# When an even chunk's k and v loads are issued in an mLSTM-plus-FFN kernel: behind the odd chunk's section, or behind the product of W's last column with v

## The chip, the core and the metric

The kernel runs on one core of a Trainium2 chip. The metric is the device time of one execution in microseconds (us). Five engines work side by side, each through its own instructions in order: TensorE (PE, with its weight loads listed as PEld), VectorE (DVE), ScalarE (ACT), GpSimd (POOL) and SyncE (SP). SP, POOL and ACT also issue DMAs, each through a queue of its own; an issue stands in the engine's order like any other instruction.

## The reference

Two blocks follow each other. The first is an mLSTM cell over 4 batches, 8 heads, 768 tokens and a head size of 40:

```python
for t in range(S):
    m_new = np.maximum(f_gate[:, :, t] + m, i_gate[:, :, t])
    f_stab = np.exp(f_gate[:, :, t] + m - m_new)
    i_stab = np.exp(i_gate[:, :, t] - m_new)
    C = f_stab * C + i_stab * outer(v_t, k_t)
    n = f_stab * n + i_stab * k_t
    y_t = sigmoid(o_gate_t) * (C @ q_t) / max(|n . q_t|, 1)
```

The second takes y as 3072 rows of 320 numbers: `h = max(x @ w_in, 0)`, then `(h * h) @ w_out`, with w_in of 320 x 2048 and w_out of 2048 x 320. All in float32.

## The kernel before

**Chunks and groups.** The attention is done in 24 chunks of 128 tokens (six to a batch, all heads at once), numbered s; c is s modulo 6. Two chunks make one group g of 256 token rows for the FFN, so there are 12 groups. In the steady part (the loop of lines 1437 to 1612) each stage has four steps, `at` = 0 to 3. In an even stage s the second FFN product of an old group runs (`ffn2_fast`, line 1063, the matmuls of L1058); in an odd stage s the first FFN product of a later group runs in two halves (`ffn1_open`, `ffn1_close` and `ffn1_rows`, lines 1142, 1175 and 1158; matmuls L1137 and L1170). The attention of the chunks is threaded between them. The order on every engine is the order in which the program writes its instructions, since a manual schedule is set (line 87); nothing reorders them.

**One half of the first FFN product.** It uses four PSUM tiles X, Y, V and Z. `ffn1_open` fills X (L1150), Y, V and Z; ACT copies X (L1151), DVE adds that to Y (L1153, "r_sb") and then V to the sum (L1155). `ffn1_close` adds a second product to X and then writes new products over Y and V; in the second half (`at` = 3) these start afresh, so PE may write Y only when L1153 has read it, and V only when L1155 has.

**The attention of an even chunk s+1 inside odd stage s, from chunk 10 on** (`joined`). All of it comes at `at` = 2, between the two halves of the FFN product, and just behind: `weigh` lets ACT turn the masked decays A into the weights W, eight activations of L510, and then calls `values`: POOL multiplies v by the last column of W into vw (L531), which the state update needs. `weighted` then lets DVE multiply the scores by W, in place (two instructions of L609); the product is written over W, so it waits until POOL has read W's last column. Next on DVE come L1153 and L1155 of the half that was just opened, then `scale_q` (L763) and `turn_kq` (L406, a transpose). The matmuls of the chunk (`attend_begin`: L801, L821, L832) stand on PE between V's second product and the rows of L1170.

There is no vw in a batch's last chunk (c = 5), and no decay of a state in its first (c = 0).

**POOL in an odd stage.** In order: the causal mask of chunk s+1 (two L479) and the decay of the state (`decay_C`, L768, "Cd"), both at `at` = 1; then k and v of chunk s+3 (`load`, seven DMAs: L363, two of L365, four of L375), for s above `EARLY` = 10; vw of chunk s+1 (L531); eight DMAs that copy k and q of two later chunks into rows of a DRAM buffer (`pair_up`, L343; four in stage 19); k and v of chunk s+4 (seven DMAs again). Then in even stage s+1: mask and Cd of chunk s+2, vw of chunk s+2, and four subtractions and additions of x (`sums_of_x`, L1129 and L1132). DMAs of the POOL queue use eight semaphores in turn, so each waits, before it is issued, until the DMA eight places before it has landed.

**Buffers.** There are four buffers each for k and q (`kq_b`) and v (`va_b`), used in turn, so chunk s+3 is loaded into the buffers of chunk s-1. The loads of even chunks 14 to 22, those that the change touches, wait for no engine in the built program, only for their semaphore. Chunk s+3's v is first read in stage s+2.

Of the kernel before, what the change touches and what calls it, by code (L numbers as in the profile page):

```python
# [29 lines left out]
def kernel(  # L30
# [317 lines left out]
    def load(s):  # L348
        b, c = divmod(s, NB)
        (dk, sk), nat_q, vv = load_parts(s)  # L350
        if s < ROT:
            for dst, src in ((dk, sk), nat_q, vv) if s < KQ_SQ else ((dk, sk), vv):
                nc.sync.dma_start(dst, src[b, :, c * P : (c + 1) * P, :].rearrange("h p d -> p h d"))
            return
        load_k(s)
        load_v(s)
# [35 lines left out]
    def load_squares(s, eng=None):  # L392

        eng = eng or nc.sync
        t = kqT(s)[:].rearrange("p n j (m a) -> p (n j m) a", a=SQ)
        for i in range(2):
            for e in range(0, D, SQ):
                w = min(SQ, D - e)
                eng.dma_start(
                    t[DP * i + e : DP * i + e + SQ, :, :w],  # L400
                    kq_d[s, i, :, :, :, e : e + w].rearrange("n j (m r) a -> r (n j m) a", r=SQ),
                )
# [5 lines left out]
    def load_o(s):  # L408
        b, c = divmod(s, NB)
        r, (s0, s1) = next((r, (a, z)) for r, (a, z) in enumerate(RUNS) if a <= s < z)  # L410
        if s == s0:
            st["og", r] = ld.tile([P, 4, H, D], F32, name="og")
        og = st.setdefault(s, {})["og"] = st["og", r][:, s - s0]
        nc.sync.dma_start(og, o_gate[b, :, c * P : (c + 1) * P, :].rearrange("h p d -> p h d"))
# [151 lines left out]
    def scores(s, o=(False, False)):  # L566
        d = st[s]

        sc = [bank(o[i]) for i in range(2)]
        d["sc"] = sc  # L570
        if s >= KQ_SQ:
            if s >= ROT:
                d["sc"] = [t.rearrange("p j t -> p (j t)")[:, : 3 * P].rearrange("p (e t) -> p e t", e=2) for t in sc]
            for e in range(2):
                for late_keys in range(2):
                    for c in range(2):
                        for i in range(2):
                            rows = slice(DP * i, DP * i + D)
                            start = e == late_keys == 0
                            if s < ROT:  # L580
                                j, keys = 2 * late_keys + e, HALVES[c]
                                to, t0 = sc[i][HALVES[c], j, :], 0
                            else:
                                j, keys = 2 * (c ^ late_keys) + e, HALVES[late_keys]
                                to = d["sc"][i][HALVES[c], e, slice(0, DP) if late_keys else slice(DP, 3 * DP)]
                                t0 = DP * late_keys
                            nc.tensor.matmul(  # L587
                                to, lhsT=d["kT"][rows, j, keys], rhs=d["qT"][rows, j, t0:], start=start, stop=True,
                                skip_group_check=True,
                            )  # L590
            return
        for j in range(PR):
            for i in range(2):
                rows = slice(DP * i, DP * i + D)
                nc.tensor.matmul(
                    sc[i][:, j, :], lhsT=d["kT"][rows, j, :], rhs=d["qT"][rows, j, :], start=True, stop=True,
                )
# [328 lines left out]
    def store_rows(s):  # L926
        t = st[s]["xT"] = xT_half(s).rearrange("p c t -> p (c t)")
        nc.sync.dma_start(x_d[s].rearrange("c t d -> t c d"), st[s]["x"][:].rearrange("p (c d) -> p c d", c=3))

    def load_rows(s):  # L930
        t = st[s]["xT"]
        for r in range(P // SQ):
            nc.sync.dma_start(
                t[r * SQ : (r + 1) * SQ].rearrange("p (b a) -> p b a", a=SQ),
                x_d[s, :, :, r * SQ : (r + 1) * SQ].rearrange("c (n p) a -> p (c n) a", p=SQ),
            )

    def turn_squares(s):
        t = st[s]["xT"]
        nc.vector.transpose(t, t)  # L940
        del st[s]
# [86 lines left out]
    def sums_of_weights(i):  # L1028
        if i < 3:
            T[i] = late.tile([P, NPAIR, DH], F32, name=f"T{i}", bufs=1)[:]  # L1030
        if i == 0:
            nc.vector.tensor_tensor(T[0], B12, B11, op=ALU.subtract)
        elif i == 1:
            nc.vector.tensor_tensor(T[1], B22, T[0], op=ALU.subtract)
        elif i == 2:
            nc.vector.tensor_tensor(T[2], B21, T[1], op=ALU.subtract)
        else:

            nc.vector.tensor_tensor(B12, B22, B12, op=ALU.subtract)
# [118 lines left out]
    def ffn1_rows(g, q, first):  # L1158
        xT, xs = st["xT", g], st["xs"]
        X, Y, V, Z = st["f1"]  # L1160
        lo, hi = HALVES
        pairs = (
            ((X, lo, xT[lo, 0, 2, :], False), (Y, hi, xT[hi, 1, 2, :], first)),
            ((V, lo, xT[lo, 1, 2, :], first), (Z, hi, xs[hi, 1, :], False)),
        )
        for pair in pairs:
            for n in range(4):
                for cols in HALVES:
                    for to, rows, rhs, start in pair:
                        nc.tensor.matmul(  # L1170
                            to[cols, n, :], lhsT=w_in2[rows, 4 * q + n, cols], rhs=rhs,
                            start=(start and n == 0), stop=True, skip_group_check=True,
                        )
# [36 lines left out]
    def do(f, s):  # L1210
        if 0 <= s < NT:
            f(s)
# [97 lines left out]
    for u in range(8):  # L1310
        s = 2 + u // 2
# [119 lines left out]
    EARLY = 10  # L1431
    assert ROUNDED[-1] == len(pieces)

    def joined(s):
        return EARLY <= s < NT and s % 2 == 0

    for n, (which, g, i) in enumerate(parts):
        s, at = NB + n // 4, n % 4
# [3 lines left out]
        even = s % 2 == 0  # L1442
# [17 lines left out]
        if at == (0 if joined(s) else 1):  # L1460
            if not joined(s):
                do(attend_begin, s)
            if n == 5:
                sums_of_weights(3)
            if even:
                do(lambda s: scores(s, ("h" if s < EARLY else False, "h")), s + 1)
            if fast:
                ffn1_rows(g, 0, True)
                if joined(s + 1):
                    scores(s + 1, (False, "h"))  # L1470
            do(attend_end, s)
            do(decays, s + 1)
            if not even and s + 2 > EARLY:
                do(lambda s: load_squares(s, nc.scalar), s + 2)
                if s > EARLY + 1:
                    do(half_tanh, s)
            do(mask, s + 1)
            if not even and not fast:
                do(turn_kq, s + 1)
            do(decay_C, s + 1)  # L1480
            if not fast and not even:
                do(turn_squares, s - 1)
            if s == NB + 2:
                load(s + 3)
            if not even and s > EARLY:
                do(load, s + 3)
            do(store_num, s)
            if s > NB + 1:
                do(load_A, s + 2)
            if joined(s):  # L1490
                load_rows(s - 1)
            if n == 1:
                normalise_turned(5)
                store_rows(5)
                turn_squares(4)
            if n == 5:
                load_rows(6)
            do(load_num, s)
            if n == 1:
                load_rows(5)  # L1500
                weigh(7, masked=True)
                sums_of_win(2)
            if s + 2 <= EARLY:
                do(load_squares, s + 2)
            if even and s <= NB + 1:
                do(load_A, s + 2)
# [87 lines left out]
        if n in (5, 6):  # L1594
            load(4 + n)
            load_o(5 + n)
        if at == 3 and s == NB + 2 or at == 2 and joined(s + 1):
            for r in (3, 4) if even else (4, 5):
                do(pair_up, s + r)
# [43 lines left out]
```

## Time and profile before

| | us |
|---|---|
| median of 3 runs | 493.96 (492.89 to 493.99) |
| the profiled execution, its own time | 492.39 |
| its span, first to last instruction | 490.7 |
| outside the span | 1.69 |
| PE busy | 474.2 (97% of the span) |
| PEld busy | 442.6 (90%) |
| DVE busy | 346.3 (71%) |
| ACT busy | 243.6 (50%) |
| POOL busy | 223.1 (45%) |
| granted TensorE clock | 1.000 |

All times of an instruction are counted from the span's start. The views used are: the page's shares and its groups by line; the list of waits of one engine (who waited for whom, total us, times, longest); the chain of work that ended last, in order of time; and the timelines of single engines. In a timeline a row has start, duration, engine, line, operation, output<-input and count, and in brackets the idle time before it and what ended that. The odd stages that the change touches lie at about these times, by their weigh activations (L510) on ACT: stage 11 at 191.1, 13 at 227.8, 15 at 266.3, 17 at 304.8 and 19 at 341.9 us.

### The profile page before, as it was taken

What the parts mean: (1) busy time and instruction counts of PE and PEld (TensorE: products, weight loads), DVE (VectorE), ACT (ScalarE), POOL (GpSimd) and SP (SyncE); (2) the same over time, 40 slices, a digit from 0 to 9 for tenths busy, and PEclk for the clock granted to TensorE, in tenths of its full rate; (3) what the DMA queues carried; (4) which work ended last, traced back from release to release, by engine and by line L of the source; (5) the groups of instructions that cost most, each with busy time, mean ns of one, the idle gap of its engine ahead of it and who ended that gap; (6) DMA issues with size and microseconds to landing.
All of it is one profiled execution on the core that took longest, in us unless ns stands there. A gap on an engine that the chain in (4) does not pass through costs nothing.

```text
span 490.7 us, 15678 instructions
## 1 busy us (share of the span) xinstructions
PE 474.2 (97%) x6389; PEld 442.6 (90%) x6389; DVE 346.3 (71%) x725; ACT 243.6 (50%) x534; POOL 223.1 (45%) x337
## 2 busy tenths in 40 slices
PE   8989999999999999999899899999899999999997
PEld 4876787789998999999899899899899999999997
DVE  7868868898975966864966867856866867735441
ACT  4698898636645424545345453554552651514300
POOL 5464454658598735735834825824832111020000
PEclk9999999999999999999999999999999999999999
DMA  8999998689999848767867867855954322200000
GB/s 177 231 242 267 254 231 219 189 149 199 164 198 200 158 128 173 158 127 154 146 146 150 156 147 124 189 132 112 179 126 88 89 76 73 56 23 15 2 28 27
DMA packets 192839, 69.93 MB, mean 143 GB/s; under 512 B 158144, under 2 KB 181504, under 8 KB 192768
## 3 DMA queue, kind: packets, MB, share of 16 engines
q1 hardware_dynamic: 157424, 56.39, 51.9%
q0 software_dynamic: 6080, 10.16, 9.7%
q10 hardware_dynamic: 29264, 2.39, 4.5%
q8 instruction: 50, 0.82, 0.8%
q14 instruction: 21, 0.17, 0.2%
HBM read 55.69 MB, written 18.92 MB: 152 GB/s over the span
## 4 chain that ended last, share of the span: by engine, by line
PE 73%; DMA 8%; DVE 6%; POOL 4%; SPq 3%; issue 3%; ACT 2%; DVEq 0%; POOLq 0%; ACTq 0%
PE h_ps L1058 31%; PE h_ps L1137 16%; PE h_ps L1170 7%; PE h_ps L974 4%; PE h_ps L1012 4%; PE numT L821 3%; DMA kqT<-kq_rows 2%; PE numT L801 2%; POOL va L375 1%; PE tp L587 1%; DMA x_rows<-x_sb 1%; PE numT L832 1%; DMA lent_t<-in_moe_w_in_dram 1%; DMA num_rows<-tn 1%; PE h_ps L985 1%
## 5 line engine op out<-in xcount | busy, mean ns | idle before, releaser
L1074 DVE TENSOR_TENSOR y_sb<-y_sb,h_ps 128x160 f32<-128x160 f32 x44 | 13.8, 314 | 53.7 <-PE h_ps L1058 53.7
L1058 PE MATMUL h_ps<-T,S 128*128 128x160 f32 x352 | 51.4, 299 | 0.0
L1058 PE MATMUL h_ps<-w_out,g 128*128 128x160 f32 x336 | 48.9, 301 | 0.9 <-issue 0.9
L1058 PEld LDWEIGHTS h_ps<-T,S 128*128 128x128 f32 x352 | 49.0, 190 | 0.0
L1058 PEld LDWEIGHTS h_ps<-w_out,g 128*128 128x128 f32 x336 | 46.2, 190 | 2.1 <-issue 1.7
L1137 PE MATMUL h_ps<-lent_t,w_in 128*128 128x128 f32 x320 | 42.7, 276 | 5.0 <-DVE r_sb L1153 5.0
L1137 PEld LDWEIGHTS h_ps<-lent_t,w_in 128*128 128x128 f32 x320 | 38.9, 192 | 5.7 <-DVE r_sb L1153 5.7
L1151 ACT COPY r_sb<-h_ps 128x512 f32<-128x512 f32 x20 | 11.7, 584 | 65.1 <-PE h_ps L1137 65.1
L1137 PE MATMUL h_ps<-xT,w_in 128*128 128x128 f32 x320 | 43.3, 278 | 0.0
L1170 PE MATMUL h_ps<-xT,w_in 64*64 64x128 f32 x960 | 40.3, 272 | 1.4 <-DVE r_sb L1153 1.4
L1129 POOL TENSOR_TENSOR lent_t<-xT 128x128 f32<-128x128 f32 (+1 forms) x18 | 10.3, 592 | 67.0 <-DVE xT L940 67.0
L1137 PEld LDWEIGHTS h_ps<-xT,w_in 128*128 128x128 f32 x320 | 39.2, 192 | 1.6 <-issue 1.2
L375 POOL DMA_DIRECT2D va<-in_v_dram x64 | 39.2, 622 | 0.1
L1137 PE MATMUL h_ps<-lent_t 128*128 128x128 f32 x320 | 39.0, 275 | 0.0
L1170 PEld LDWEIGHTS h_ps<-xT,w_in 64*64 64x64 f32 x960 | 35.4, 133 | 2.6 <-DVE r_sb L1153 2.1
L1137 PEld LDWEIGHTS h_ps<-lent_t 128*128 128x128 f32 x320 | 37.3, 192 | 0.0
L510 ACT ACTIVATE A_bc<-A_bc,b_R 128x64 f32<-128x64 f32 (+1 forms) x128 | 35.6, 363 | 0.9 <-POOL A_bc L479 0.9
L479 POOL TENSOR_SCALAR_AFFINE_SELECT A_bc<-A_bc 64x512 f32<-64x512 f32 x32 | 23.6, 736 | 23.6 <-ACT kq L497 22.3
L1188 ACT ACTIVATE g<-h_ps 128x512 f32<-128x512 f32 x12 | 7.2, 597 | 49.2 <-PE h_ps L1170 19.5
L768 POOL TENSOR_TENSOR Cd<-C,kq 128x164 f32<-128x164 f32 x15 | 13.9, 929 | 36.2 <-DVE C L862 31.6
L974 PE MATMUL h_ps<-xT,w_in 128*128 128x256 f32 x128 | 29.9, 386 | 0.4 <-POOL w_in L236 0.4
L855 DVE STREAM_TRANSPOSE tn<-numT 128x256 f32<-128x256 f32 x36 | 14.0, 426 | 22.9 <-PE numT L801 15.7
(231 smaller groups left out, 1210.1 us busy)
## 6 DMA issues: line engine op xcount, KB each, us to landing
A_bc<-a_slots SPq DMA_DIRECT2D x32, 256.0 KB, 5.0
kq<-num_rows SPq DMA_DIRECT2D x80, 64.0 KB, 3.1
num_rows<-tn SPq DMA_DIRECT2D x18, 256.0 KB, 2.9
raw<-in_moe_w_out_dram SPq DMA_DIRECT2D x7, 640.0 KB, 4.7
og<-in_o_gate_dram SPq DMA_DIRECT2D x24, 160.0 KB, 4.9
x_rows<-x_sb SPq DMA_DIRECT2D x20, 192.0 KB, 2.7
xT<-x_rows SPq DMA_DIRECT2D x80, 48.0 KB, 3.5
out_dram<-y_sb SPq DMA_DIRECT2D x23, 160.0 KB, 2.3
```

What stands on the lines that cost most here:

```text
L375: eng.dma_start(dst[HALVES[n], PR * (1 - late_keys) : PR * (2 - late_keys)], src[HALVES[late_keys], PR * m : PR * (m + 1)],)
L479: nc.gpsimd.affine_select(part, part, compare_op=ALU.is_ge, fill=-1e30, base=0, pattern=[[0, PR], [0, 2], [1, DP]], channel_multiplier=-1,)
L510: nc.scalar.activation(A[0][:, x, to], A[0][:, x, to], AF.Exp, bias=b_R[:, b, c, own, x : x + 1],)
L768: nc.gpsimd.tensor_tensor(Cd, C_b[(s - 1) % 2][:, : PR * D1].rearrange("p (j d) -> p j d", d=D1), st[s]["eA"][:, :, P - 1 : P].to_broadcas ...
L821: nc.tensor.matmul(d["numT"][m][HALVES[e], i, t0:], lhsT=va_w[s % NKQ][keys, at * D1 : at * D1 + DP], rhs=rhs, start=(s % NB == 0 and i == ...
L855: nc.vector.transpose(to[:, 2 * m : 2 * m + 2], d["numT"][m].rearrange("p c t -> p (c t)"))
L974: nc.tensor.matmul(hs[i][:, n, :], lhsT=w_in[:, a, fb * P : (fb + 1) * P], rhs=xT[:, :, a, :], start=(n == 0 and a == 0), stop=False,)
L1012: nc.tensor.matmul(st["o_ps"][j], lhsT=st["g2", 0][:, fb, j * P : (j + 1) * P], rhs=w_out[:, fb, :], start=(fb == 0), stop=(fb == NF - 1),)
L1058: nc.tensor.matmul(to, lhsT=lhsT[:, p], rhs=rhs[:, p, :], start=(start and p == 0), stop=(p == NPAIR - 1), skip_group_check=True,)
L1074: add = lambda to, a, b: nc.vector.tensor_tensor(to, a, b, op=ALU.add)
L1137: nc.tensor.matmul(to[:, n, :], lhsT=lhsT[:, 4 * q + n, :], rhs=rhs, start=(start and n == 0), stop=True, skip_group_check=True,)
L1170: nc.tensor.matmul(to[cols, n, :], lhsT=w_in2[rows, 4 * q + n, cols], rhs=rhs, start=(start and n == 0), stop=True, skip_group_check=True,)
```

## The change

In odd stages above 10 the call that loads k and v of chunk s+3 moves from `at` = 1 (behind mask and Cd of chunk s+1) to the end of `at` = 2, behind vw of chunk s+1 and ahead of the copies of `pair_up`. It holds for s = 11, 13, 15, 17 and 19, that is for the chunks 14, 16, 18, 20 and 22.

```diff
             if s == NB + 2:
                 load(s + 3)
-            if not even and s > EARLY:
-                do(load, s + 3)
             do(store_num, s)
...
         if n in (5, 6):
             load(4 + n)
             load_o(5 + n)
+        if at == 2 and not even and s > EARLY:
+            do(load, s + 3)
         if at == 3 and s == NB + 2 or at == 2 and joined(s + 1):
             for r in (3, 4) if even else (4, 5):
                 do(pair_up, s + r)
```

The instructions of PE, DVE, ACT and SP keep their order. On POOL one instruction changes places with seven, five times:

```diff
 L768 TensorTensor Cd<-C_1208,kq_94 128x164
-L363 DMACopy kq_92<-in_k_dram 128x4x40
-L365 DMACopy kq_92<-in_k_dram 64x4x40 x2
-L375 DMACopy va_96<-in_v_dram 64x4x40 x4
-L531 TensorTensor vw<-va_98,A_bc 128x328
+L531 TensorTensor vw<-va_98,A_bc 128x328
+L363 DMACopy kq_92<-in_k_dram 128x4x40
+L365 DMACopy kq_92<-in_k_dram 64x4x40 x2
+L375 DMACopy va_96<-in_v_dram 64x4x40 x4
 L343 DMACopy kq_rows<-in_k_dram 16x4x320 x2
 L343 DMACopy kq_rows<-in_q_dram 16x4x320 x2
```

The order of POOL's DMAs among themselves is the same, and so are the semaphores that they use.

## The prediction

> **What bounds the kernel now.** I read the page's shares first, then who makes PE wait in the steady part, then who makes that engine wait, then the chain.
>
> ```profile
> PE 474.2 (97%) x6389; PEld 442.6 (90%) x6389; DVE 346.3 (71%) x725; ACT 243.6 (50%) x534; POOL 223.1 (45%) x337
> ```
>
> PE is busy 97% of the span, with a full granted clock, so time is won only where PE stands still. The waits of PE and of DVE between 150 and 400 us:
>
> ```profile
> PE h_ps L1137 <- DVE r_sb L1153: 5.0, 4, 1.3
> ```
> ```profile
> DVE A_bc L609 <- POOL vw L531: 5.9, 3, 2.0
> ```
>
> PE waits four times for L1153, the DVE instruction that reads Y. In three of the four, DVE itself stood about 2 us in front of L609 until POOL had made vw. The chain of waits shows what POOL did meanwhile, here in stage 13:
>
> ```profile
> 227.44 0.46 POOL Cd L768
> 227.90 0.79 POOL kq L363
> 228.69 1.23 POOL kq L365 x2
> 229.91 2.43 POOL va L375 x4
> 232.36 0.77 POOL vw L531
> 233.19 0.44 issue
> 233.62 0.55 DVE A_bc L609
> 234.17 0.61 DVE r_sb L1153
> 234.82 2.05 PE h_ps L1137 x16
> ```
>
> It issued the seven loads that the change moves, 4.46 us, while W was ready long before vw began: ACT's timeline has the last L510 done at 227.82 + 2.22 = 230.04. The same chain stands at 265.96 (stage 15) and 341.56 (stage 19). Stages 11 and 17 differ: their chunk is a batch's first, no Cd holds the loads back, and ACT is last. POOL's timeline of stage 17:
>
> ```profile
> 297.82 0.80 POOL L363 DMA_DIRECT2D kq<-in_k_dram  x1 [0.50 <-issue]
> 298.62 1.23 POOL L365 DMA_DIRECT2D kq<-in_k_dram  x2
> 299.84 2.45 POOL L375 DMA_DIRECT2D va<-in_v_dram  x4
> 307.20 0.74 POOL L531 TENSOR_TENSOR vw<-va,A_bc 128x328 f32<-128x328 f32 x1 [4.92 <-ACT A_bc L510]
> ```
>
> These two stages are my model of the changed ones: vw starts 0.14 us behind ACT (304.84 + 2.22 = 307.06), L609 goes on right behind DVE's L940, and PE has no gap there.
>
> **What the change takes away, stage 13.** POOL is free after Cd at 227.90, ACT ready at 230.04, so vw starts at 230.18 and ends at 230.92 (0.74, as in stage 17). DVE is busy until then: L1192 at 230.02, L940 at 230.62 to 231.19; in stage 17 L609 starts 0.49 us after L940 starts, so here at 231.11, not 233.15. L1153, 0.94 us behind it in stage 13 (234.09 - 233.15), starts at 232.05 and ends at 232.73. PE's second Y may begin one block, 0.90 us, behind the second X at 232.48, that is at 233.38; L1153 is 0.65 us early. L1155, 0.78 us behind L1153, ends at 233.52; the second V needs it at 234.27. L763, 1.39 us behind L1153, ends at 234.12; the chunk's matmuls (L801) need it at 236.81 - 1.55 = 235.26. Nothing on DVE is late next.
>
> **Price of the stall.** On PE's timeline, from the start of the second X to the start of the second V:
>
> ```profile
> 309.50 1.06 PE L1137 MATMUL h_ps<-xT,w_in 128*128 128x128 f32 x8
> 310.40 1.06 PE L1137 MATMUL h_ps<-lent_t,w_in 128*128 128x128 f32 x8
> 311.29 1.06 PE L1137 MATMUL h_ps<-xT,lent_t 128*128 128x128 f32 x8
> ```
>
> 1.79 us in stage 17, without a stall. In stage 13 it is 235.82 - 232.48 = 3.34, in stage 15 274.35 - 270.98 = 3.37, in stage 19 349.94 - 346.58 = 3.36. The stalls cost 1.55 + 1.58 + 1.57 = 4.70 us. Stages 11 and 17 give 0: vw cannot be earlier than ACT.
>
> **What the change puts later.** On POOL the seven issues (4.47 us) now stand behind vw, and behind them, as before, the eight `pair_up` copies, the seven loads of chunk s+4, and mask and Cd of chunk s+2. The other queues (SP's and ACT's) are passed by nothing. The even chunk's data is late for nobody: chunk 16's last issue would end at 235.4 instead of 232.3, at most 7.4 us to landing (the longest of the 64 v loads) makes 242.8, and vw of chunk 16 reads it near 270. The rows of `pair_up` in stage 13 are first read back in stage 15, near 258.
>
> What could be late is the mask, since each copy waits for the DMA eight places before it. In stage 13 of before the sixth copy started at 236.72, released by the landing of the second v load, issued by 231.1: 5.6 us to land. I use that for all, as these stages are the busy ones for DMA. Stage 11, the tightest: vw ends at 193.49 + 0.74 = 194.23; loads 4.47, to 198.7; the eighth copy waits for the last load, to 204.3, and takes 0.51; loads of chunk 15 4.44, to 209.3; mask 1.56, to 210.8, against 204.8 before. ACT would like to start L510 of chunk 13 at 209.29, so it is 1.7 us late there. But its 2.23, 0.14 and a slow vw of 1.21 bring vw to 214.5, and DVE takes up L609 of chunk 13 at 216.36: 1.8 us of slack left, cost 0. Even with 7.4 us to land the mask ends at 212.6 and vw at 216.3.
>
> The others have more, with PE's earlier times taken off: stage 13's mask ends at 247.5 (before 244.4), L609 of chunk 15 is due at 255.56 - 1.55 = 254.0, and 247.5 + 0.14 + 2.23 + 0.14 + 1.21 = 251.2 leaves 2.8. Stage 17 ends its mask 6.6 us later than before but keeps about 3; stages 15 (next chunk has no vw) and 19 (four copies, not eight) keep 4 or more. So this costs 0 as long as landings stay below about 7.5 us.
>
> Two bounds are open. **vw's own time** beside a busy DVE: L531 took 738 to 1206 ns. At 1.21 it ends at 231.39, L1153 at 233.06, still 0.3 early: cost 0. The longest vw in the trace, 1.76 us (the form of L537), would put L1153 at 233.6, 0.25 late, or 0.75 us in three stages. **The issues** beside a busy DVE: 64 L375 took 617 to 654 ns while DVE was busy 71%, so I take no stretch.
>
> A rule speaks against this last point. The Trainium skill, "SBUF — State Buffer", section "A bandwidth-pool intuition that's wrong (but worth ruling out)", has a DMA issued by GpSimd take about 3.1 us instead of 0.62 beside a VectorE copy that holds their shared port. The loads move from beside an idle DVE to beside a busy one. By that rule one such issue in a stage, 2.5 us longer, would eat stage 12's 1.8 us and cost 0.7, making the sum -4.0 us. This trace shows no stretched issue.
>
> **Sum.** -4.70 + 0 + 0 = -4.7 us. The profiled execution took 492.39 in its own time (span 490.7), which becomes 487.7. The median of the runs is 493.96, 1.57 above it; I forecast for a median: **489.3 us**. The spread of the three runs (1.1 us), below and above, with a few tenths for small shifts elsewhere, makes its own range 487.6 to 490.6. About 0.3% (1.5 us) is what a measurement of this kernel can tell from no change.
>
> **Rivals.**
>
> *Part of the gain is given back* (chance 0.08): vw is slower than 1.2 us beside DVE, or the delayed mask holds ACT in stage 12 alone. For it: the slow vws stand beside DVE work, and stage 12's slack is the smallest. Against: at 1.21 and at 7.4 us both are still covered. Price: 0.75 us by the 1.76 row, up to 2.5 us with landings near 10 us in one stage: 490.0 to 491.8.
>
> *Nothing is won: the wait for vw isn't the cause* (chance 0.08). L609 would next wait for another thing that came at nearly the same time (the scores, or a DMA behind L940), as in the fourth L1153 stall at 159.65, where vw was done at 156.93 and DVE went on late only behind L940, released by the DMA of xT. For it: that one case. Against: in all three stages L940 was done 2 us before vw and the profile names vw. Two of three stalls staying leaves -1.6; all three, 0: 492.4 to 494.
>
> *Slower: POOL's shifted queue holds the even stages* (chance 0.04). Place: the mask of chunks 13, 15, 19 and 21, then L510, vw and L609 in stages 12, 14, 18 and 20. Point: landings 1.8 us above 5.6 in stage 12, about 3 above in stages 14 and 18. From there each us is a us of PE. At 10 us to landing, 4.4 above, that is 2.6 + 1.6 + 1.4 + 0 = 5.6 against 4.7 won: 494.9; at 12 us, 4.6 + 3.6 + 3.4 = 11.6, 500.9. Against it: the longest landing of a v load is 7.4 and their median 4.2.
>
> **Numbers.** The forecast has 0.80. The range, 487.6 to 491.8, takes the forecast and the first rival: 0.88, some of it cut at the tails. Both lie below 493.96 - 1.48 = 492.48, so faster has 0.88; the second rival is what lies within 0.3%, 0.08; the third is slower, 0.04.
>
> **What would show it.** Right: no wait of L609 for vw in stages 13, 15 and 19; second X to second V 1.8 us there; L1137's 5.0 us of idle near 1.3; the mask of chunk 13 near 210.8 and L609 of chunk 13 still near 216.4. Wrong: L609 named with another releaser at the old time; ACT's L510 of chunks 13, 15, 19 or 21 so late that L609 waits for vw in an even stage; issues of L363 to L375 longer than 0.8 us.

## The result, and the profile after

The changed kernel takes 488.38 us (median of 4 runs, 487.65 to 490.26) against 493.98 us (492.89 to 494.66, 4 runs) in the same comparison: ratio 0.9895, 95% interval 0.9861 to 0.9928. Of 494 us that is 5.2 us less, by the interval 3.6 to 6.9. Here and below a gain in us is worked out from the ratio; the plain difference of the two medians can be other by some tenths (here it is 5.6). The profiled execution took 487.65 us (span 485.9) against 492.39 (span 490.7).

The page's shares of the changed kernel, and then who made PE wait between 150 and 400 us (total us, times, longest):

```profile
PE 474.5 (98%) x6389; PEld 442.6 (91%) x6389; DVE 343.3 (71%) x725; ACT 244.3 (50%) x534; POOL 220.6 (45%) x337
```
```profile
PE h_ps L1170 <- DVE r_sb L1153: 1.1, 2, 0.6
...
PE h_ps L1137 <- DVE r_sb L1153: 0.2, 1, 0.2
```

PE's busy time is the same (474.2 before). The 5.0 us of L1137 in four waits are 0.2 us in one, and that one is the old stall at 160 us, outside the change, which differs from execution to execution. The row of DVE's waits that named vw (5.9 us, 3 times) is gone.

Stage 13 of the changed kernel, POOL's timeline and then DVE's (start, us, engine, line, operation, in brackets the idle time before and what ended it):

```profile
230.66 0.75 POOL L531 TENSOR_TENSOR vw<-va,A_bc 128x328 f32<-128x328 f32 x1 [2.21 <-ACT A_bc L510]
231.35 0.80 POOL L363 DMA_DIRECT2D kq<-in_k_dram  x1
232.15 1.23 POOL L365 DMA_DIRECT2D kq<-in_k_dram  x2
233.37 2.45 POOL L375 DMA_DIRECT2D va<-in_v_dram  x4
```
```profile
231.16 0.57 DVE L940 STREAM_TRANSPOSE xT<-xT 128x384 f32<-128x384 f32 x1
231.66 0.52 DVE L609 TENSOR_TENSOR A_bc<-tp,A_bc 128x384 f32<-128x384 f32 x1
232.10 0.54 DVE L609 TENSOR_TENSOR A_bc<-h_ps,A_bc 128x384 f32<-128x384 f32 x1
232.56 0.68 DVE L1153 TENSOR_TENSOR r_sb<-h_ps,r_sb 128x512 f32<-128x512 f32 x1
```

vw now waits for ACT instead of standing behind seven issues, and L609 follows L940 without a gap. In the profile of before the same L609 waited for vw:

```profile
233.15 0.56 DVE L609 TENSOR_TENSOR A_bc<-tp,A_bc 128x384 f32<-128x384 f32 x1 [1.96 <-POOL vw L531]
```

The last blocks of PE's half, its second X, Y and V:

```profile
233.03 1.06 PE L1137 MATMUL h_ps<-xT,w_in 128*128 128x128 f32 x8
233.93 1.06 PE L1137 MATMUL h_ps<-lent_t,w_in 128*128 128x128 f32 x8
234.82 1.06 PE L1137 MATMUL h_ps<-xT,lent_t 128*128 128x128 f32 x8
```

From second X to second V it is 1.79 us, where it was 3.34. Stage 15 (269.45 to 271.24) and stage 19 (343.24 to 345.02) show 1.79 and 1.78. So the three stalls gave back 1.55 + 1.58 + 1.58 = 4.71 us.

The start of one block of PE's matmuls in each of several stages, by the chain of waits of each kernel, shows what else moved (the first block of the stage, but in stage 17 the one behind the first rows of L1170):

| start, us | before | after | after minus before |
|---|---|---|---|
| stage 12, L1058 | 202.35 | 203.17 | +0.82 |
| stage 14, L1058 | 241.56 | 240.03 | -1.53 |
| stage 16, L1058 | 279.56 | 276.45 | -3.11 |
| stage 17, L1137 | 303.22 | 300.11 | -3.11 |
| stage 20, L1058 | 355.15 | 350.23 | -4.92 |
| stage 22, L1058 | 392.20 | 387.45 | -4.75 |

The 0.82 is there before stage 11, where the two kernels are alike. From stage 12 to 22 the difference is 5.57 us: the 4.71 of the stalls, and 0.86 in small gaps of PE that the profile names "issue" (0.41 and 0.31 us ahead of L832 in the profile of before are two of them); these come and go between executions of one kernel (a second profile of the changed kernel has 0.28 us ahead of L832, this one none).

The delayed queue of stage 11, in POOL's timeline (mask of chunk 13, its Cd and vw), ACT's and DVE's:

```profile
210.12 1.42 POOL L479 TENSOR_SCALAR_AFFINE_SELECT A_bc<-A_bc 64x512 f32<-64x512 f32 x2
211.62 0.46 POOL L768 TENSOR_TENSOR Cd<-C,kq 128x164 f32<-128x164 f32 x1
213.88 0.75 POOL L531 TENSOR_TENSOR vw<-va,A_bc 128x328 f32<-128x328 f32 x1 [1.80 <-ACT A_bc L510]
```
```profile
211.57 2.23 ACT L510 ACTIVATE A_bc<-A_bc,b_R 128x64 f32<-128x64 f32 x8 [1.35 <-POOL A_bc L479]
```
```profile
212.34 0.68 DVE L763 TENSOR_TENSOR kq<-kq,kqT 128x512 f32<-128x512 f32 x1
...
217.18 0.52 DVE L609 TENSOR_TENSOR A_bc<-tp,A_bc 128x384 f32<-128x384 f32 x1
```

The mask ends at 211.54; with the 0.82 taken off, 210.7 in the time of before. ACT is 1.35 us late, vw ends at 214.63, and L609 starts at 217.18 as in before (216.36 + 0.82). L763 starts at 212.34, 0.26 us after Cd has ended; that number matters further down. (A second profile of the changed kernel has 0.76 us there; no copy waited for a landing in it.)

### The profile page after: what moved, and what is told of

Same layout as the page of the kernel before. It is cut to its first block, busy times and chain, and to the rows that moved or that the text cites. A ratio compares the mean times of both kernels' runs of the same rounds, so it can differ in the third digit from the quotient of the medians.

```text
span 485.9 us, 15678 instructions
## 1 busy us (share of the span) xinstructions
PE 474.5 (98%) x6389; PEld 442.6 (91%) x6389; DVE 343.3 (71%) x725; ACT 244.3 (50%) x534; POOL 220.6 (45%) x337
## 4 chain that ended last, share of the span: by engine, by line
PE 74%; DMA 11%; DVE 5%; SPq 3%; ACT 3%; POOL 2%; issue 2%; DVEq 0%; POOLq 0%; ACTq 0%
PE h_ps L1058 31%; PE h_ps L1137 21%; PE h_ps L1170 7%; PE h_ps L974 3%; DMA A_bc<-a_slots 3%; PE numT L821 2%; PE numT L801 2%; DMA og<-in_o_gate_dram 2%; DMA raw<-in_moe_w_out_dram 1%; PE tp L587 1%; PE numT L832 1%; DMA xT<-x_rows 1%; DMA kqT<-kq_rows 1%; PE tp L555 1%; SPq L399 1%
## 5 line engine op out<-in xcount | busy, mean ns | idle before, releaser
L1074 DVE TENSOR_TENSOR y_sb<-y_sb,h_ps 128x160 f32<-128x160 f32 x44 | 13.9, 315 | 54.4 <-PE h_ps L1058 54.4
L1058 PE MATMUL h_ps<-T,S 128*128 128x160 f32 x352 | 51.4, 299 | 0.0
L1058 PE MATMUL h_ps<-w_out,g 128*128 128x160 f32 x336 | 48.9, 301 | 0.7 <-issue 0.7
L1058 PEld LDWEIGHTS h_ps<-T,S 128*128 128x128 f32 x352 | 49.0, 190 | 0.0
L1058 PEld LDWEIGHTS h_ps<-w_out,g 128*128 128x128 f32 x336 | 46.2, 190 | 1.9 <-issue 1.3
L1137 PE MATMUL h_ps<-xT,w_in 128*128 128x128 f32 x320 | 43.3, 278 | 0.0
L1137 PE MATMUL h_ps<-lent_t,w_in 128*128 128x128 f32 x320 | 42.4, 275 | 0.2 <-DVE r_sb L1153 0.2
L1170 PE MATMUL h_ps<-xT,w_in 64*64 64x128 f32 x960 | 40.3, 272 | 1.6 <-DVE r_sb L1153 1.6
L1137 PEld LDWEIGHTS h_ps<-xT,w_in 128*128 128x128 f32 x320 | 39.2, 192 | 1.6 <-issue 1.2
L1137 PEld LDWEIGHTS h_ps<-lent_t,w_in 128*128 128x128 f32 x320 | 38.9, 192 | 0.4 <-DVE r_sb L1153 0.4
L375 POOL DMA_DIRECT2D va<-in_v_dram x64 | 39.2, 619 | 0.0
L1129 POOL TENSOR_TENSOR lent_t<-xT 128x128 f32<-128x128 f32 (+1 forms) x18 | 10.3, 593 | 63.5 <-DVE xT L940 63.5
L1137 PE MATMUL h_ps<-lent_t 128*128 128x128 f32 x320 | 39.1, 275 | 0.0
L1170 PEld LDWEIGHTS h_ps<-xT,w_in 64*64 64x64 f32 x960 | 35.4, 133 | 2.8 <-DVE r_sb L1153 2.4
L1137 PEld LDWEIGHTS h_ps<-lent_t 128*128 128x128 f32 x320 | 37.3, 192 | 0.2 <-issue 0.2
L479 POOL TENSOR_SCALAR_AFFINE_SELECT A_bc<-A_bc 64x512 f32<-64x512 f32 x32 | 25.2, 787 | 23.1 <-ACT kq L497 21.8
L1189 DVE TENSOR_TENSOR r_sb<-r_sb,h_ps 128x512 f32<-128x512 f32 x20 | 13.8, 688 | 22.4 <-PE h_ps L1137 12.0
```

The source lines that it names most:

```text
L375: eng.dma_start(dst[HALVES[n], PR * (1 - late_keys) : PR * (2 - late_keys)], src[HALVES[late_keys], PR * m : PR * (m + 1)],)
L479: nc.gpsimd.affine_select(part, part, compare_op=ALU.is_ge, fill=-1e30, base=0, pattern=[[0, PR], [0, 2], [1, DP]], channel_multiplier=-1,)
L1058: nc.tensor.matmul(to, lhsT=lhsT[:, p], rhs=rhs[:, p, :], start=(start and p == 0), stop=(p == NPAIR - 1), skip_group_check=True,)
L1074: add = lambda to, a, b: nc.vector.tensor_tensor(to, a, b, op=ALU.add)
L1129: sub = lambda to, a, b: eng.tensor_tensor(to, a, b, op=ALU.subtract)
L1137: nc.tensor.matmul(to[:, n, :], lhsT=lhsT[:, 4 * q + n, :], rhs=rhs, start=(start and n == 0), stop=True, skip_group_check=True,)
```

## The experiments

All were timed against the kernel before on the same chip, but on three chips in all, so the ratios can be compared with each other and the times can't. The theory T: the gain is only the three waits of L609 for a late vw, and POOL's shifted queue is covered. The rivals: the wait for vw isn't the cause; the queue costs.

**The move in stages 13, 15 and 19 alone.** Against the changed kernel:

```diff
+            if s in (11, 17, 21, 23, 25):
+                do(load, s + 3)
...
-        if at == 2 and not even and s > EARLY:
+        if at == 2 and s in (13, 15, 19):
             do(load, s + 3)
```

> The move is made in stages 13, 15 and 19 only; stages 11 and 17 keep the loads ahead of vw. Theory (the loads stand on POOL between Cd and vw, and L609 waits for vw, in these three stages alone): the whole gain of the changed kernel, 4.7 us against before (ratio 0.990 to 0.991), and second X to second V 1.8 us in all three. Rival (each of the five moves helps alike, for instance by spreading DMA traffic): three fifths of what the changed kernel won, 2.8 to 3.4 us (ratio 0.993 to 0.994).

Measured: 486.39 us against 491.40, ratio 0.9894 (0.9870 to 0.9918). The whole gain is in these three stages.

**The move in stages 11 and 17 alone.** The same edit, with the two lists of stages exchanged.

> The move is made in stages 11 and 17 only. Theory: 0 (ratio 0.998 to 1.002), the three waits of L609 for vw stay near 2.0 us each and PE's idle before L1137 near 5.0 us. Rival (all five alike): two fifths of the gain, 1.9 to 2.2 us (ratio 0.996).

Measured: 491.10 us against 491.40, ratio 0.9995 (0.9980 to 1.0010). DVE's and PE's waits stay:

```profile
DVE A_bc L609 <- POOL vw L531: 6.0, 3, 2.0
```
```profile
PE h_ps L1137 <- DVE r_sb L1153: 4.8, 4, 1.3
```

Together the two runs split the change: all of it in the stages that have a Cd and a vw, nothing in the two that wait for ACT.

**Two of the four v loads moved, and only the last one moved.** `load_most(s, n)` issues all but the last n loads of v at the old place, the rest go to the new place:

```diff
+            if not even and s > EARLY:
+                do(lambda s: load_most(s, 2), s + 3)
...
-            do(load, s + 3)
+            do(lambda s: load_v(s, range(2, 4)), s + 3)
```

> Only the last two of the seven DMAs (two quarters of v) move behind vw, in all five stages; five stay ahead of it. Theory: vw starts 1.22 us earlier than before in stages 13, 15 and 19 (two issues of 0.61), L609 too, and 0.35 us of each stall of 1.57 is left: 3.7 us won (ratio 0.992 to 0.993), PE idle before L1137 about 1.0 us in those stages together. Rival (gain in proportion to the DMAs that move): two sevenths of 4.7 to 5.6, 1.3 to 1.6 us (0.997).

> Only the last of the seven DMAs (one quarter of v) moves behind vw, six stay ahead. Theory: vw and L609 come 0.61 us earlier than before in stages 13, 15 and 19, 0.96 us of each stall of 1.57 is left: 1.8 us won (ratio 0.996), and with two moved DMAs 3.7, so each DMA is worth its issue on POOL. Rival (in proportion to the DMAs): 0.7 to 0.8 us (0.998 to 0.999).

Measured for two: 487.77 us against 491.40, ratio 0.9925 (0.9902 to 0.9948), that is 3.7 us. Measured for one: 492.10 against 493.41, ratio 0.9979 (0.9960 to 0.9998), 1.0 us, with 0.1 to 2.0 by the interval. The waits for vw in DVE's list, first with two moved, then with one (the lines are shifted by 6: L615 is L609, L537 is L531):

```profile
DVE A_bc L615 <- POOL vw L537: 2.3, 3, 0.8
```
```profile
DVE A_bc L615 <- POOL vw L537: 4.1, 3, 1.4
```

The wait is 5.9, 4.1, 2.3 and 0 us with none, one, two and all seven loads moved out of vw's way. Each of the first two takes 1.8 us off in three stages, 0.6 us a stage, which is one L375 (619 ns). With one load moved, PE's idle time ahead of the second Y is 0.68, 0.70 and 0.71 us, where it was 1.28, 1.32 and 1.31: 1.82 us less, as T has it, though the time by itself would not have told T's 1.8 from the rival's 0.7.

**vw from a copy of the column; the loads stay at the old place.** ACT copies W's last column for the even chunks, so nobody who writes over W waits for POOL:

```diff
+                if s % 2 == 0 and s > 11:
+                    own_last = prep.tile([P, 2, PR], F32, name="own_last")
+                    nc.scalar.copy(own_last[:], last)
+                    last = own_last[:]
```

> All loads stay where before has them, ahead of vw; for the even chunks from 12 on ACT copies W's last column (128 x 8) into a small tile right behind L510, and POOL makes vw from the copy, so L609 waits for ACT's copy and no longer for vw. vw itself stays 2 us late in stages 13, 15 and 19. Theory (late vw costs only through L609, which may not write over W before POOL has read it): nearly the whole gain, 4.2 to 4.7 us against before (ratio 0.990 to 0.992), less what the copy puts between L510 and L1151, about 0.3 us, which L1153 has to spare. Rival (PE needs vw itself, in L832, or something else holds DVE): 0 to 1.5 us (0.997 to 1.0).

Measured: 489.14 us against 493.41, ratio 0.9906 (0.9878 to 0.9934), 4.6 us. POOL's and DVE's timelines in stage 13 (lines shifted by 4: L535 is vw, L613 is L609):

```profile
235.23 0.75 POOL L535 TENSOR_TENSOR vw<-va,own_last 128x328 f32<-128x328 f32 x1
```
```profile
233.97 0.52 DVE L613 TENSOR_TENSOR A_bc<-tp,A_bc 128x384 f32<-128x384 f32 x1
```

vw is as late as before behind the loads, and DVE no longer cares. This is the sharpest test of the cause: with POOL's order untouched, taking the write-over-W dependency away gives nearly the same gain, 4.6 us for 5.2, with intervals that overlap. That vw wasn't the cause is excluded.

**The loads ahead of the mask.** Issued at `at` = 0 of the odd stage, where POOL would otherwise be idle, instead of behind vw:

```diff
+        if at == 0 and not even and s > EARLY:
+            do(load, s + 3)
...
-        if at == 2 and not even and s > EARLY:
-            do(load, s + 3)
```

> The loads go the other way: to the start of the odd stage, ahead of the mask and Cd of chunk s+1 on POOL, so that they are earlier than in before and still not between Cd and vw. Theory (place in POOL's order counts, not the time of the transfers): the same gain as the changed kernel, 4.7 us against before (0.990 to 0.991), and no wait of ACT's L510 for a late mask in stage 12. Rival (it helps that these transfers come later, away from others): no gain or less than 2 us, with transfers landing later than 5.6 us.

Measured: 485.39 us against 491.40, ratio 0.9864 (0.9840 to 0.9888), 6.7 us and more than T's 4.7. The rival is excluded: in stages 13, 15 and 19 these transfers come earlier than in before, the v loads land after 4.5 us in the median (4.2 in before), and the gain is there. As for what it won beyond T, two waits of L1170 for L1153, 0.57 us each, are gone. They come from DVE where stage 10 turns into 11 and stage 16 into 17, and before has them too (1.1 us in its list of waits). DVE's timeline of the changed kernel at the second of these places, and what POOL did:

```profile
292.40 1.17 DVE L896 TENSOR_TENSOR x_sb<-kq,og 128x128 f32<-128x128 f32 x2
293.49 0.75 DVE L898 TENSOR_TENSOR x_sb<-kq,og 128x32 f32<-128x32 f32 x2
```
```profile
292.71 1.50 POOL L479 TENSOR_SCALAR_AFFINE_SELECT A_bc<-A_bc 64x512 f32<-64x512 f32 x2
```

With the loads first the mask comes at 298.50, and the two pairs take 0.70 and 0.28 us: 0.94 us less on DVE ahead of L1153. The next run tests that reading.

**The mask later, by memsets.** The changed kernel with eight memsets ahead of the masks of chunks 12 and 18:

```diff
+            if s in (11, 17):
+                for _ in range(8):
+                    nc.gpsimd.memset(spare[:], 0.0)
             do(mask, s + 1)
```

> The changed kernel, with about 1.5 us of memsets on POOL ahead of the mask of chunks 12 and 18 in stages 11 and 17 only. The kernel with early loads won about 1 us more than the changed one, and there DVE's L896 and L898 in front of stages 11 and 17 took 0.70 and 0.28 us instead of 1.17 and 0.75, as POOL's mask (L479) no longer ran beside them. Theory of that extra gain (the mask beside L896 and L898 slows them, so that L1153 comes 0.94 us late for L1170): L896 and L898 at 0.70 and 0.28, no idle of PE before L1170 (1.1 us in the changed kernel), 1.2 to 1.9 us faster than the changed kernel (ratio 0.986 to 0.987 against before). Rival (the extra gain comes from the earlier transfers, or POOL's memsets slow L896 as well): as the changed kernel (0.9895) or slower.

Measured: 487.53 us against 493.41, ratio 0.9877 (0.9848 to 0.9907). DVE's and POOL's timelines at the same place:

```profile
292.36 0.70 DVE L896 TENSOR_TENSOR x_sb<-kq,og 128x128 f32<-128x128 f32 x2
292.99 0.28 DVE L898 TENSOR_TENSOR x_sb<-kq,og 128x32 f32<-128x32 f32 x2
```
```profile
292.65 1.83 POOL L1480 MEMSET spare<- 128x96 f32 x8
```

A memset beside the same DVE instructions leaves them at the time that they have with the loads first; the mask does not. L1170's waits are gone as well. The time fits the extra 1.1 us but doesn't show it, since the interval holds the changed kernel's 0.9895 too.

**Both again on one chip.**

> The changed kernel itself, once more, beside the version with the loads ahead of the mask on the same chip. Theory: 4.7 us less than before, ratio 0.9895 to 0.991.

> The loads at the start of the odd stage, ahead of the mask, once more. Theory: the 4.7 us, and two times about 0.6 us more, since the mask no longer runs beside the four DVE instructions L896 and L898 in stages 10 and 16 and L1170 no longer waits for L1153: ratio 0.002 to 0.003 below that of the changed kernel in the same call. Rival (the first run's lower time was spread): the same ratio as the changed kernel.

Measured: the changed kernel 488.45 us, ratio 0.9881 (0.9847 to 0.9916); the loads ahead of the mask 488.19 us, ratio 0.9868 (0.9830 to 0.9907), both against 494.26. The difference has the expected sign and half the expected size, and the intervals overlap almost entirely. In the profile of the early loads L1170's waits are gone again, but 0.87 and 0.38 us of "issue" gaps ahead of L832 stand where the changed kernel of the same call has 0.28. So the early place is at least as good; that it is better than the changed kernel isn't shown.

**POOL's queue delayed on purpose.** The changed kernel with 20 memsets ahead of the loads of chunk s+4 in stages 11 to 21, which delays mask, Cd, vw and the sums of x in the even stages:

```diff
+        if at == 3 and joined(s + 1) and s > EARLY:
+            for _ in range(20):
+                nc.gpsimd.memset(spare[:], 0.0)
         if at == 3 and (s == NB + 2 or joined(s + 1)):
             do(load, s + 4)
```

> The changed kernel, with some 3.8 us of memsets on POOL (20 of 128 x 96, on a tile that nobody reads) ahead of the loads of chunk s+4 in stages 11 to 21, so that the mask, Cd and vw of the next even stage come 3.8 us later. Theory, from the changed kernel's trace: L609 of chunk 13 comes 2.5 us behind vw there, of chunk 15 about 3.5, of chunk 19 about 3.3, of chunk 21 more, and chunk 17 has no vw; so 1.3 + 0.3 + 0.5 + 0 + 0 = 2.1 us against the changed kernel, that is 2.6 us faster than before (ratio 0.993 to 0.996), with L609 waiting for vw in even stages. Rival 1 (POOL's shifted queue is off the path altogether): as the changed kernel, 0.9895. Rival 2 (there is no slack left): five times 3.8, 19 us, slower than before (1.03).

Measured: 493.17 us against 493.41, ratio 0.9999 (0.9974 to 1.0024). The memsets took 4.70 us a stage, and all of the gain is gone: 5 us against the changed kernel, where T expected 2.1. L609 waits for no vw in any even stage, so the reckoning of the prediction (mask, ACT, vw, L609) isn't what costs. DVE's and PE's timelines in stage 12:

```profile
215.64 0.69 DVE L763 TENSOR_TENSOR kq<-kq,kqT 128x512 f32<-128x512 f32 x1 [4.00 <-POOL Cd L768]
```
```profile
216.62 2.44 PE L1058 MATMUL h_ps<-w_out,S 128*128 128x160 f32 x16 [0.99 <-DVE y_sb L1074]
218.89 1.05 PE L1137 MATMUL h_ps<-xT,w_in 128*128 128x128 f32 x8
220.15 2.05 PE L1137 MATMUL h_ps<-lent_t 128*128 128x128 f32 x16 [0.21 <-POOL lent_t L1132]
```

L763, which scales in place what Cd reads, waits for Cd. Behind it on DVE stand the sums of the FFN's output (L1074), for which PE waits 0.99 us, and L940, for which the sums of x on POOL wait, and for those PE again. By the starts of L1058, PE loses 1.7 us from stage 12 to 14, 0.5 from 14 to 16, 2.3 from 16 to 20 and 0.35 from 20 to 22, 4.8 against the changed kernel.

**The same delay behind Cd.** The 20 memsets stand in the even stages now, behind mask and Cd and ahead of vw:

```diff
             do(decay_C, s + 1)
+            if even and s > EARLY:
+                for _ in range(20):
+                    nc.gpsimd.memset(spare[:], 0.0)
```

> The 20 memsets (4.7 us a stage) stand behind mask and Cd of the even stages' chunks, ahead of vw and of the sums of x; mask and Cd are on time. Theory (the delay of POOL cost so much because Cd came late, DVE's scale_q L763 waits for Cd, with 0.2 us to spare in stage 12, and everything of DVE behind it comes late): no wait of L763 for Cd; vw of chunk 13 starts near 216.9 and L609 waits about 0.5 us for it, the sums of x end 0.2 us late for PE; about 0.2 to 0.5 us in each of three stages, so 0.6 to 1.5 us of the gain given back, ratio to before 0.990 to 0.993. Rival (it was the late vw and the late sums of x, or the memsets beside DVE): as much given back as before, ratio 0.997 to 1.001.

Measured: 487.53 us against 494.26, ratio 0.9863 (0.9832 to 0.9893): nothing is given back, even less than T expected. POOL's and DVE's timelines in stage 12:

```profile
211.01 0.46 POOL L768 TENSOR_TENSOR Cd<-C,kq 128x164 f32<-128x164 f32 x1
211.41 4.66 POOL L1484 MEMSET spare<- 128x96 f32 x20
216.04 0.75 POOL L531 TENSOR_TENSOR vw<-va,A_bc 128x328 f32<-128x328 f32 x1
```
```profile
211.80 0.69 DVE L763 TENSOR_TENSOR kq<-kq,kqT 128x512 f32<-128x512 f32 x1
```

With Cd on time L763 doesn't wait, and vw, 2.7 us later than in the changed kernel (it would start at 213.88 - 0.54, by the start of L763), just meets L609 at 216.82. So the vw path has about 2.5 us to spare, as reckoned, and the delay cost so much by way of Cd. The mask and the loads of chunk s+4 are on time here as well, so this run alone doesn't tell them from Cd; that it is Cd rests on the wait of L763 that the kernel with the delayed queue shows (11.6 us in four stages by DVE's list of waits).

## Why the prediction was right, point by point

- **The bound and the stall's price** held. 4.70 us was forecast for the three stalls, 4.71 went. The profiled execution came to 487.65 us for a forecast of 487.7. That this agrees to 0.05 us is luck: the 0.82 us lost ahead of stage 11 and the 0.86 us of gaps that went cancel each other. The median came to 488.38 for 489.3, within the range.
- **The model of the changed stages** held to a tenth: vw starts 0.07 us behind ACT (228.37 + 2.22 = 230.59; 0.14 reckoned) and takes 0.75 us; L609 starts 0.50 us behind L940's start; L1153 0.90 us behind L609 (0.94 reckoned). Nothing on DVE was late next: L763 stands at 233.95.
- **Nothing in stages 11 and 17**: held by the second experiment (0.9995).
- **The issues beside a busy DVE** took no longer: 2.45 us for four L375 beside L1153, L1155 and L763, 619 ns in the mean of all 64. The stretch that the prediction weighed, a DMA issue held up by a VectorE copy, is not seen; the DVE instructions beside the moved issues are no plain copies, so this kernel doesn't test it.
- **The delayed mask**: 210.8 was forecast and 210.7 came, ACT 1.35 us late for 1.7. The agreement is partly luck. The landings were shorter than the 5.6 us assumed (in stage 11 the last two copies waited for the landing of the third v load, issued by 200.4, until 204.67, that is 4.2 us; the copies of stage 13 were held up 0.15 us in all, where before they waited 0.73 and 0.28 us for landings), and the first load of stage 11 came late instead, by an "issue" gap of 1.45 us that no row of before shows behind a vw.
- **The step that was incomplete** is the one on POOL's queue: "What could be late is the mask". The prediction followed mask, ACT, vw and L609, and found 1.8 us of slack; after the change that path had about 2.5. But Cd stands behind the mask too, L763 on DVE waits for Cd, and there the slack in stage 12 was 0.26 us (0.76 in the second profile). A queue later by more than that would have held up DVE. The cost of 0 was still right, because behind L763 PE has some 3 us more: in the delayed kernel L763 came 4.1 us late in stage 12, and PE waited 0.99. The sentence "cost 0 as long as landings stay below about 7.5 us" rested on the wrong path, and so did the rival's price of one us of PE for each us of delay: 4.7 us in each of six stages cost 4.8 in all by the profile.
- **The rivals**: that vw isn't the cause was excluded by the copied column. That the shifted queue costs was excluded by the stage table and the first two experiments. A slow vw didn't come either: beside DVE it took 0.74 to 0.75 us in stages 13, 15 and 19.
- The measured 5.2 us are more than 4.7, as in the repeat (5.9), but 4.7 lies in each interval. The 0.86 us beyond the stalls in the profile are "issue" gaps; that they belong to the change isn't shown.

## What to carry to other kernels

On an engine that works in order and also issues DMAs, an issue is an instruction like any other (here 0.5 to 0.8 us): place a batch of them where the next instruction behind them isn't waited for, and price the move by how far the late instruction reaches, which here was one tile written in place (W) and from there PE. When a queue is made later, follow every instruction in the delayed stretch to its readers and over-writers, not only the last of the chain that you are mending: here the small product in the middle (Cd) had 0.3 us to spare before DVE waited for it, and the one at the end (vw) 2.5. If a tile that is written over in place couples two engines, a copy of the few columns needed (0.20 us on ACT) can be worth nearly as much as a new order, as it was here.

## What the runs showed of the hardware

- **The mask on POOL and two-input instructions on DVE lengthen each other.** Beside L479 the pairs L896 and L898 took 1.17 and 0.75 us, beside memsets 0.70 and 0.28. (Even 0.70 isn't the time alone: the last L1129 on POOL overlaps it, and where POOL only issued DMAs, in stages 12 and 14 of the changed kernel, L896 took 0.44.) The other way round, the two L479 took 2.29 us in stage 14 and 2.75 in stage 16, beside L1053, against 1.42 in stage 12, and L1053 took up to 1.64 in stage 16 for 1.21. The Trainium skill, "SBUF — State Buffer", section "SBUF: two separate sides", has a VectorE instruction with two SBUF inputs and a GpSimd instruction that reads SBUF exclude each other on a shared port pair. The difference between mask (reads SBUF) and memset (only writes) agrees with that rule.
- **A gap ahead of the first DMA issue.** In stage 11 the first L363 started 1.45 us after vw had ended, named "issue", in the changed kernel and in the delayed one alike, and 1.35 us in stage 17. In stages 13, 15 and 19 there is no such gap ahead of L363, and none behind vw in stages 11 and 17 of before, where a copy of `pair_up` came next. In the two stages with the gap POOL had stood idle for 9.9 us ahead of vw, in the other three for 2.2. What sets it stays open; it delays a covered queue and cost nothing here.
